# Two weight loads moved among the first rows, an earlier start of weight decoding, and four row loads moved to ScalarE, in an attention and two-layer feed-forward kernel

## The chip, the cores and the metric

The kernel runs on one core of one Trainium2 chip. Its five engines each work through a queue of their own in order: TensorE (PE; its weight loads are shown as PEld), VectorE (DVE), ScalarE (ACT), GpSimd (POOL) and SyncE (SP), which here only issues DMAs. The metric is the device time of one execution in microseconds. Three runs of the kernel before gave 977.05 us as their median (972.66 to 978.73).

## The reference

```python
def _attn_ref(q, k, v):                       # 4 batches, 8 heads, 576 positions, 64 wide
    # out_up: attention among means of 4 positions, repeated 4 times
    # out_local: attention of each position to those less than 4 away
    return (out_up + out_local).astype(np.float32)

x = attn_out.transpose(0, 2, 1, 3).reshape(2304, 512)
h = x @ w_in;  x = (h * sigmoid(h)) @ w_out          # w_in 512 x 2048, w_out 2048 x 512
h = x @ w_in2; out = elu(h) @ w_out2                 # the second layer, same sizes
```

Queries and keys are drawn about six times larger than a tenth of a normal draw. The weights come as 64-bit floats, read here as pairs of 32-bit words.

## The kernel before, in words

A *pair* is two heads of one batch, four pairs to a batch. `attention(i)` is a generator that does one pair in 19 steps: the rows of queries and keys are transposed on TensorE (tile `pst`, L297) and copied to SBUF by ScalarE (L305, L307); the local scores (`psl`, L319) get the mask on VectorE (L326) and their maxima are taken off on GpSimd (`E`, L334); the averaged scores (`psd`, L363) go through exponentials on ScalarE (L377), the local ones too (L383); sums and reciprocals come from VectorE, the products with them from GpSimd; the weights are transposed again (`psE`, `psD`, copies `aT` L406 and `aD` L415 on ScalarE), multiplied with the values (`psu` L422, `pso` L434) and added up in `x32` (L425 ScalarE, L442 VectorE).

A *weight* here is one tile of 128 x 512 numbers, 512 KB as it comes. `load_next` issues its DMA on SP into one of three staging buffers (`ws`). `decode_w` makes a 32-bit float of it: two ScalarE operations (L157, L159), three of VectorE (L168, L169, L175); after the third, the staging buffer is free and the next load is issued. `split_w` cuts it into a high and a low part (ScalarE cast L185, GpSimd L187). The first 16 weights, eight of `w_in` and eight of `w_out` in turn, are all that the first pass of the first layer needs. They are prepared by `prepare_first`, six calls of `small_first` for a weight.

Before the first product of the feed-forward part, a loop runs the four pairs of the first batch (`pending(0)`), counting their steps in `n`. From the thirteenth step on (L722) each step also adds 1.1 to `early`, and every whole unit of it is one call of `small_first`. After that loop come the blocks of 256 tokens. A *unit* is one block with one of eight slices f: `g1` makes `ph` (L501), ScalarE takes the tanh (L518), VectorE the product (L520), ScalarE the high part `gh` (L528), GpSimd the low part; `g2` (L565) follows three units later. The remaining pairs are stepped between the products by `tick`, but only once all 16 first weights have been begun (`first["next"] == 2 * FP`), and what is left of the first weights is stepped there too.

The order on each queue is the order of the code (`manual_schedule`). On SP that is: queries and keys of pairs 0 to 3, the first weight, values of pair 0, the second weight, values of pair 1, the third weight, values of pairs 2 and 3; then each further weight when its buffer is free. Keys of pairs 0 and 1 are issued by ScalarE. Rows of pair 4, the first of the second batch, are loaded by `load_pair` within pair 3's sixth step (L344), on SP.

Every DMA takes the next of eight completion semaphores, in the order of the program whichever engine issues it, and its issue waits until the DMA that had this semaphore before has landed. Below these are called lanes; in lists with waits they are named `DMAHW0` to `DMAHW7`.

Of the kernel before, what the change touches and what calls it, by code (L numbers as in the profile page):

```python
# [22 lines left out]
def attention_moe_moe2_kernel(ctx, tc, q, k, v, wi1, wo1, wi2, wo2, out):  # L23
    nc = tc.nc
# [7 lines left out]
    NPAIR = H // 2  # L32
# [21 lines left out]
    EARLY_PACE = 1.1  # L54
# [73 lines left out]
    def load_next():  # L128
        if at["load"] < len(order):
            load_w(at["load"])  # L130
            at["load"] += 1

    def load_w(i):
        layer, f, which = order[i]
        src = wsrc[layer][which].bitcast(I32)
        st = stage.tile([P, 2 * DM], I32, tag="ws", name="ws", bufs=3)
        if which == 0:
            nc.sync.dma_start(
                st.rearrange("p (c f) -> p c f", c=KC),
                src[:, f * 2 * P:(f + 1) * 2 * P].rearrange("(c p) f -> p c f", p=P),  # L140
            )
        else:
            nc.sync.dma_start(st, src[f * P:(f + 1) * P, :])
        wst[i] = st
# [59 lines left out]
    def load_rows(i, which, engine=None):  # L204
        b, h0 = pairs[i][0], 2 * pairs[i][1]
        src = (q, k, v)[which]
        if which == 2:

            if i < NPAIR:
                heads = [wpool.tile([P, DM], F32R, tag=tag, name="rows2").bitcast(F32) for tag in ("wh0", "wl0")]  # L210
            else:
                t = nat.tile([P, 4 * FAC * D], F32, tag="natv", name="rows2", bufs=1)
                heads = [t[:, :DM], t[:, DM:]]
            for j, t in enumerate(heads):
                (engine or nc.sync).dma_start(t[:HS], src[b, h0 + j].rearrange("(p r) d -> p (r d)", r=2 * FAC))
            loaded[i, which] = heads
            return

        if i in (1, 2):
            ts = [xs.tile([P, NBM], F32R, tag=("xh", "xl")[which], name=f"rows{which}", bufs=6).bitcast(F32) for _ in range(2)]  # L220
            half = NTB // 2
            for j in range(2):
                for a in range(2):
                    (engine or nc.sync).dma_start(
                        ts[a][:TB, :half * 2 * D].rearrange("p (c e) -> p c e", c=half)[:, :, j * D:(j + 1) * D],
                        src[b, h0 + j].rearrange("(c p) d -> p c d", p=TB)[:, a * half:(a + 1) * half],
                    )
                borrowed[2 * i - 2 + which, j] = ts[j]
            loaded[i, which] = [t[:, c * 2 * D:(c + 1) * 2 * D] for t in ts for c in range(half)]
            return  # L230
        elif i == 3 and which == 0:
            borrowed["y"] = yp.tile([P, 4 * NBM], F32, tag="y", name="rows0")
            t = borrowed["y"]
        else:
            t = nat.tile([P, NTB * 2 * D], F32, tag="nat", name=f"rows{which}", bufs=2)
        t = t[:, :NTB * 2 * D].rearrange("p (c e) -> p c e", c=NTB)
        for j in range(2):
            (engine or nc.sync).dma_start(t[:TB, :, j * D:(j + 1) * D], src[b, h0 + j].rearrange("(c p) d -> p c d", p=TB))
        loaded[i, which] = [t[:, c] for c in range(NTB)]

    def load_windows(i):
        b, h0 = pairs[i][0], 2 * pairs[i][1]
        if i in (2, 3):
            vw = borrowed["y"][:, (i - 2) * NW * D:(i - 1) * NW * D].rearrange("p (n d) -> p n d", d=D)
        else:
            vw = nat.tile([P, NW, D], F32, tag="vw", name="vw")
        for j in range(2):
            rows = v[b, h0 + j]
            nc.sync.dma_start(
                vw[j * WIN:(j + 1) * WIN, :NW - 1, :],  # L250
                bass.AP(tensor=rows.tensor, offset=rows.offset, ap=[[D, WIN], [w0[1] * D, NW - 1], [1, D]]),
            )
            nc.sync.dma_start(vw[j * WIN:(j + 1) * WIN, NW - 1, :], rows[w0[-1]:w0[-1] + WIN, :])
        loaded[i, 3] = vw

    def warm(n):
        pz = ps_h.tile([P, 512], F32, tag="h", name="pz")
        for _ in range(n):
            nc.tensor.matmul(pz, wz[0][:, :P], wz[0][:, :512], start=True, stop=True)

    def load_pair(i):
        for which in range(3):
            load_rows(i, which)
# [18 lines left out]
    def attention(i):  # L282
# [11 lines left out]
        for parts in ([(0, c) for c in range(NTB - 1)], [(1, c) for c in range(NTB - 1)], [(0, NTB - 1), (1, NTB - 1)]):  # L294
# [4 lines left out]
            for which in range(2):  # L299
                n = TB * sum(w == which for w, _ in parts)  # L300
# [40 lines left out]
            nc.gpsimd.tensor_tensor(vt[:HS, 2 * j:2 * j + 2], vn[:HS, :, 0:2, :], vn[:HS, :, 2:4, :], ALU.add)  # L341
        nc.gpsimd.tensor_tensor(vd[:HS], vt[:HS, :, 0, :], vt[:HS, :, 1, :], ALU.add)
        if NPAIR - 1 <= i < len(pairs) - 1:
            load_pair(i + 1)  # L344
        if i >= 2:
            load_windows(i)

# [43 lines left out]
        for x, heads in EDs:  # L391
            n = heads.stop - heads.start
# [34 lines left out]
        for t in range(2):  # L427
            ps = bank("pso")
            for w in range(t * NW // 2, (t + 1) * NW // 2):
                n = a0[w + 1] - a0[w]  # L430
# [163 lines left out]

    with tc.manual_schedule():
        for i in range(NPAIR):
            load_rows(i, 0)
            load_rows(i, 1, nc.scalar if i < 2 else nc.sync)
        load_next()
        load_rows(0, 2)  # L600
        load_windows(0)
        load_next()
        load_rows(1, 2)
        load_windows(1)
        load_next()
# [49 lines left out]
        def small_first():  # L655
            live = first["live"]
            if first["next"] < 2 * FP and (sum(x[1] < 3 for x in live) < 2 and len(live) < 3):
                live.append([prepare_first(first["next"]), 0])
                first["next"] += 1
            if live:  # L660
                x = live.pop(0)
                try:
                    next(x[0])
                    x[1] += 1
                    live.append(x)
                except StopIteration:
                    pass
# [7 lines left out]
        def start_pair():  # L675
            i = state["next"]
            if i < state["limit"]:
                state["live"].append([pairs[i], attention(i), 0])
                state["next"] += 1

        def step(b=B):

            live = state["live"]
            if not live or (len(live) < state["most"] and min(x[2] for x in live) >= state["apart"]):
                start_pair()
            if not live:
                return False

            x = next((x for x in live if x[0][0] <= b), live[0])
            live.remove(x)  # L690
            try:
                next(x[1])
                x[2] += 1
                live.append(x)
            except StopIteration:
                pass
            if state["next"] == NPAIR:
                state["most"], state["apart"] = 3, 6
            return True

        def pending(b):
            return state["next"] < len(pairs) and pairs[state["next"]][0] <= b or any(x[0][0] <= b for x in state["live"])
# [6 lines left out]
        n = 0  # L709
        first_x = split_x(0, 0, 0)  # L710
        done = 0
        early = 0.0
        while pending(0):
            step()

            while done < NPAIR and state["next"] > done and pairs[done] not in [p for p, _, _ in state["live"]]:
                next(first_x)
                done += 1
            n += 1
            if n <= 16:  # L720
                warm(1)
            early += EARLY_PACE if n > 12 else 0  # L722
            while early >= 1:
                early -= 1
                if first["next"] < N_EARLY or len(first["live"]) > 1:
                    small_first()
# [48 lines left out]
        for i in range(len(units) + LAG):  # L775
            if i < len(units):
                layer, ps, n, f = units[i]
# [33 lines left out]
            if i >= LAG:  # L811
# [3 lines left out]
                layer, ps, n, f = u  # L815
# [32 lines left out]
```

## Time and profile before

| what | value |
|---|---|
| median of three runs (lowest, highest) | 977.05 us (972.66, 978.73) |
| the profiled execution, its own time | 978.92 us |
| its span, first to last instruction | 977.1 us |
| mean granted TensorE clock | 0.973 |
| PE, DVE, ACT, POOL busy | 96%, 52%, 45%, 36% of the span |

Times inside the trace count from the first instruction. The own time of the profiled execution is 1.8 us longer than its span. PE's busy share says little of the first tenth, where it waits for the other engines: the page's 40 slices show PE at 6, 5, 8 and 8 tenths in the first four (24.4 us each) and at 9 from there on, with a granted clock of 9, 6, 7 and 7 tenths.

### The profile page before, as it was taken

To read this page: it belongs to the slowest core of one execution; us is meant where nothing else is said; L and a number is where in the kernel's file an instruction comes from. 1 tells how busy PE (TensorE), PEld (TensorE's weight loads), DVE (VectorE), ACT (ScalarE), POOL (GpSimd) and SP (SyncE) were. 2 spreads that over 40 slices of the span, in tenths; PEclk is the share of its full clock that TensorE was granted. 3 is DMA by queue.
4 is the path that set the end of the run, shared out by engine and by line. 5 is a ranking of instruction groups with operands and counts; after the bars stand their busy time and mean duration, and the time that the engine had idled before them with its cause. 6 is when DMAs were issued, how large, how long until landed. Compare 5 with 4: busy or idle time off the path is not lost.

```text
span 977.1 us, 16442 instructions
## 1 busy us (share of the span) xinstructions
PE 935.5 (96%) x6493; PEld 805.0 (82%) x6493; DVE 511.7 (52%) x841; ACT 439.4 (45%) x995; POOL 353.1 (36%) x363
## 2 busy tenths in 40 slices
PE   6588999999999999999999999999999999999998
PEld 3357888999989999988888887888888888888886
DVE  4786554454446776654554367656544544434332
ACT  3686454545536666543434345434333433232221
POOL 3675544455452245322223433222233522222221
PEclk9677999999999999999999999999999999999999
DMA  9775342332212650422221103221101011112021
GB/s 181 168 191 159 85 113 70 85 93 71 79 37 87 177 169 35 126 78 87 65 66 64 44 1 87 87 87 44 65 0 44 1 65 65 44 44 86 1 87 44
DMA packets 93484, 77.60 MB, mean 79 GB/s; under 512 B 61664, under 2 KB 82144, under 8 KB 92384
## 3 DMA queue, kind: packets, MB, share of 16 engines
q1 hardware_dynamic: 91008, 75.97, 27.1%
q8 instruction: 51, 0.84, 0.4%
q10 hardware_dynamic: 2400, 0.59, 0.3%
q14 instruction: 25, 0.20, 0.1%
HBM read 62.39 MB, written 14.16 MB: 78 GB/s over the span
## 4 chain that ended last, share of the span: by engine, by line
PE 62%; ACT 1%; DVE 1%; issue 1%; DMA 0%; SPq 0%; DVEq 0%; ACTq 0%
PE ph L501 31%; PE y L567 19%; PE y L565 12%; DMA ws<-in_moe_w_out_dram 0%; DVE part L588 0%; DVE t L523 0%; ACT t L524 0%; ACT xh L462 0%; DVE xl L465 0%; ACT ws L159 0%; ACT gh L528 0%; ACT wf L157 0%; ACT wh L185 0%; DVE wf L169 0%; DVE wf L168 0%
## 5 line engine op out<-in xcount | busy, mean ns | idle before, releaser
L530 POOL TENSOR_TENSOR gl<-t,gh 128x256 fp32r<-128x256 f32 (+1 forms) x192 | 204.6, 1066 | 519.3 <-ACT gh L528 464.9
L501 PE MATMUL ph<-xh,wh 128*128 128x256 f32 (+1 forms) x768 | 252.2, 341 | 3.8 <-ACT xh L462 2.2
L501 PE MATMUL ph<-xl,wh 128*128 128x256 f32 (+1 forms) x768 | 250.9, 339 | 1.8 <-DVE xl L465 1.6
L501 PE MATMUL ph<-xh,wl 128*128 128x256 f32 (+1 forms) x768 | 179.8, 339 | 0.0
L501 PEld LDWEIGHTS ph<-xh,wh 128*128 128x128 f32 x768 | 146.5, 191 | 21.6 <-ACT xh L462 2.8
L501 PEld LDWEIGHTS ph<-xl,wh 128*128 128x128 f32 x768 | 146.5, 191 | 19.1 <-DVE xl L465 3.2
L528 ACT CAST gh<-t 128x256 fp32r<-128x256 f32 (+1 forms) x192 | 98.7, 514 | 120.2 <-DVE t L520 67.7
L565 PE MATMUL y<-gh,wh 128*128 128x256 f32 (+1 forms) x448 | 146.1, 326 | 1.3 <-DVE yo L578 1.3
L501 PEld LDWEIGHTS ph<-xh,wl 128*128 128x128 f32 x768 | 129.1, 191 | 15.3 <-issue 0.2
L565 PE MATMUL y<-gl,wh 128*128 128x256 f32 (+1 forms) x448 | 141.2, 315 | 0.0
L565 PE MATMUL y<-gh,wl 128*128 128x256 f32 (+1 forms) x448 | 141.1, 315 | 0.0
L520 DVE SCALAR_TENSOR_TENSOR t<-t,ph 128x256 f32<-128x256 f32 (+1 forms) x112 | 55.3, 494 | 160.3 <-ACT t L518 159.4
L524 ACT ACTIVATE t<-t 128x512 f32<-128x512 f32 (+1 forms) x80 | 47.1, 589 | 195.6 <-DVE t L523 195.6
L523 DVE TENSOR_SCALAR t<-ph 128x512 f32<-128x512 f32 (+1 forms) x80 | 51.0, 637 | 122.3 <-PE ph L501 121.9
L567 PE MATMUL y<-wh,gh 128*128 128x512 f32 x288 | 112.2, 390 | 0.0
L567 PE MATMUL y<-wh,gl 128*128 128x512 f32 x288 | 112.2, 390 | 0.0
L567 PE MATMUL y<-wl,gh 128*128 128x512 f32 x288 | 112.0, 389 | 0.0
L518 ACT ACTIVATE t<-ph 128x256 f32<-128x256 f32 (+1 forms) x112 | 49.6, 443 | 116.4 <-PE ph L501 113.8
L565 PEld LDWEIGHTS y<-gh,wh 128*128 128x128 f32 x448 | 86.3, 193 | 9.7 <-issue 2.1
L465 DVE TENSOR_TENSOR xl<-x,xh 128x256 fp32r<-128x256 f32 (+1 forms) x96 | 69.4, 740 | 45.1 <-ACT xh L462 43.4
L565 PEld LDWEIGHTS y<-gl,wh 128*128 128x128 f32 x448 | 86.4, 193 | 5.0
L565 PEld LDWEIGHTS y<-gh,wl 128*128 128x128 f32 x448 | 86.2, 192 | 5.0
(90 smaller groups left out, 1211.4 us busy)
## 6 DMA issues: line engine op xcount, KB each, us to landing
ws<-in_moe_w_in_dram SPq DMA_DIRECT2D x32, 512.0 KB
ws<-in_moe_w_out_dram SPq DMA_DIRECT2D x32, 512.0 KB
rows<-in_v_dram SPq DMA_DIRECT2D x36, 144.0 KB
yp<-yo SPq DMA_DIRECT2D x10, 512.0 KB
part<-yp SPq DMA_DIRECT2D x10, 512.0 KB
out_dram<-part SPq DMA_DIRECT2D x18, 256.0 KB
yp<-yo SPq DMA_DIRECT2D x4, 1024.0 KB
part<-yp SPq DMA_DIRECT2D x4, 1024.0 KB
```

The lines of the kernel that those rows point to most:

```text
L465: nc.vector.tensor_tensor(lo[c - 1], src[:, c - 1, :], hi[c - 1].bitcast(F32), ALU.subtract)
L501: nc.tensor.matmul(ph[:, :nb], a[:, c, :], b[c], start=m == 0, stop=m == 3 * KC - 1)
L518: nc.scalar.activation(t, h, AF.Tanh, scale=0.5)
L520: nc.vector.scalar_tensor_tensor(t, t, 1.0, h, op0=ALU.add, op1=ALU.mult)
L523: nc.vector.tensor_scalar_min(t, h, 0.0)
L524: nc.scalar.activation(t, t, AF.Exp)
L528: nc.scalar.copy(gh, t)
L530: nc.gpsimd.tensor_tensor(gl, t, gh.bitcast(F32), ALU.subtract)
L565: nc.tensor.matmul(y[d // share][:, h:h + nb], wm[:, sl], gm, start=first and d % share == 0, stop=last, skip_group_check=True)
L567: nc.tensor.matmul(y[d], gm[:, sl], wm, start=first, stop=last)
```

## The change

Three edits. (1) The first two weight loads stand ahead of the rows of pair 1 and of pair 2 in the start of the program; the third stays where it was. (2) `early` grows from the third step on, no longer from the thirteenth. (3) The queries and keys of pair 4 are issued by ScalarE, its values still by SP; for later pairs all stay on SP.

```diff
@@ attention(i) @@
         if NPAIR - 1 <= i < len(pairs) - 1:
-            load_pair(i + 1)
+            load_rows(i + 1, 0, nc.scalar if i < NPAIR else nc.sync)
+            load_rows(i + 1, 1, nc.scalar if i < NPAIR else nc.sync)
+            load_rows(i + 1, 2)
@@ start of the program @@
         for i in range(NPAIR):
+            if 1 <= i < 3:
+                load_next()
             load_rows(i, 0)
             load_rows(i, 1, nc.scalar if i < 2 else nc.sync)
-        load_next()
         load_rows(0, 2)
         load_windows(0)
-        load_next()
         load_rows(1, 2)
@@ loop over the first batch @@
-            early += EARLY_PACE if n > 12 else 0
+            early += EARLY_PACE if n > 2 else 0
```

Line numbers behind L344 are two higher in the changed kernel (L377 is L379 there, L383 is L385, L501 is L503).

SP's queue at the start. Before, the first weight (`ws_137`) stands behind the rows of all four pairs:

```order
L224 DMA rows1_126<-in_k_dram 96x3x64
L238 DMA rows0_131<-in_q_dram 96x6x64 x2
L238 DMA rows1_134<-in_k_dram 96x6x64 x2
L138 DMA ws_137<-in_moe_w_in_dram 128x4x256
L215 DMA rows2_139<-in_v_dram 72x512
```

In the change (`ws_107` is the first weight, `ws_121` the second, `rows0_109` and `rows0_110` are queries of pair 1, `rows0_123` of pair 2):

```order
L238 DMA rows0_101<-in_q_dram 96x6x64 x2
L138 DMA ws_107<-in_moe_w_in_dram 128x4x256
L224 DMA rows0_109<-in_q_dram 96x3x64
L224 DMA rows0_110<-in_q_dram 96x3x64
L224 DMA rows0_109<-in_q_dram 96x3x64
L224 DMA rows0_110<-in_q_dram 96x3x64
L143 DMA ws_121<-in_moe_w_out_dram 128x1024
L224 DMA rows0_123<-in_q_dram 96x3x64
```

The two weights moved ahead of 16 and 18 of SP's row loads; the third weight (`ws_159` in both) still stands behind the values of pairs 0 and 1.

ScalarE's queue behind the last copy of pair 1's transposed rows, before. `ws_137`, `ws_148` and `ws_159` are the first three weights, L377 the exponentials of pair 0 (`rows0_107`, `rows0_108`), L383 those of its local scores, `pst_355` to `pst_417` rows of pair 2:

```order
L307 COPY x32_98<-pst_315 128x96
L377 ACTIVATE rows0_107,sm_301<-psd_305,nm_311 72x144 x2
L305 ACTIVATE x32_98<-pst_355 128x480
L377 ACTIVATE rows0_108,sm_301<-psd_306,nm_324 72x144 x2
L381 ACTIVATE sm_301<-sm_301 72x4
L157 ACTIVATE pw_369<-ws_137 128x512
L159 ACTIVATE ws_137<-ws_137 128x512
L307 COPY x32_98<-pst_377 128x480
L157 ACTIVATE pw_386<-ws_148 128x512
L159 ACTIVATE ws_148<-ws_148 128x512
L383 ACTIVATE E_247<-E_247 128x640
L305 ACTIVATE x32_98<-pst_417 128x96
```

In the change, from the last copy of pair 1 on (`ws_159` is the third weight, `rows0_109` and `rows0_110` are pair 0's exponentials, `pst_380` and `pst_406` pair 2's rows, `ws_295` is the fourth weight):

```order
L305 ACTIVATE x32_98<-pst_332 128x96
L307 COPY x32_98<-pst_332 128x96
L157 ACTIVATE pw_339<-ws_159 128x512
L159 ACTIVATE ws_159<-ws_159 128x512
L379 ACTIVATE rows0_109,sm_315<-psd_319,nm_325 72x144 x2
L305 ACTIVATE x32_98<-pst_380 128x480
L185 CAST wh1_391<-wf_348 128x512
L379 ACTIVATE rows0_110,sm_315<-psd_320,nm_344 72x144 x2
L383 ACTIVATE sm_315<-sm_315 72x4
L307 COPY x32_98<-pst_406 128x480
L385 ACTIVATE E_250<-E_250 128x640
L157 ACTIVATE pw_419<-ws_295 128x512
```

The third weight moved ahead of all of pair 0's exponentials and of pair 2's copies, which stood before it; the first two weights are decoded and the first is cast ahead of this place.

ScalarE's queue at the loads of pair 4, in the change, with waits (`wh0_667` is the cast of the seventh weight, `ws_581` the ninth weight, L427 is L425 of before, the copy of pair 0's upsampled part):

```order
L408 COPY aT_653<-psE_659 128x384 [waits PE_49,Activation_49]
L385 ACTIVATE E_464<-E_464 128x640
L185 CAST wh0_667<-wf_643 128x512 [waits DVE_49]
L238 DMA rows0_677<-in_q_dram 96x6x64 [waits DMAHW1_49]
L238 DMA rows0_677<-in_q_dram 96x6x64 [waits DMAHW3_49]
L238 DMA rows1_680<-in_k_dram 96x6x64 [waits DMAHW5_49,DMAHW0_49]
L238 DMA rows1_680<-in_k_dram 96x6x64 [waits DMAHW0_49]
L157 ACTIVATE pw_702<-ws_581 128x512 [waits DMAHW4_49]
L159 ACTIVATE ws_581<-ws_581 128x512
L427 COPY x32_98<-psu_709 128x576
```

Before, these four DMAs stood on SP between the ninth weight's load and the values of pair 4, and ScalarE went from the seventh weight's decoding to L425. In the change, lane 5 of the third DMA was last given to the load of the tenth weight, lane 0 of the fourth to the first window load of pair 3, which SP issues three DMAs after that weight.

## Rows read from the trace of the kernel before

**Rows 1.** The page's first line: span and instructions.
```profile
span 977.1 us, 16442 instructions
```
**Rows 2.** Windows: stretch and its length; busy PE, PEld, DVE, ACT, POOL; clock; DMA.
```profile
31.15:52.89 21.74, 15.12 (x125) 9.51 (x125) 15.54 (x28) 15.61 (x44) 13.97 (x16) 0.66 0.65 167
52.89:74.08 21.19, 16.60 (x210) 11.68 (x207) 18.79 (x37) 19.20 (x48) 14.48 (x15) 0.79 0.72 173
74.08:96.16 22.08, 18.41 (x151) 16.83 (x152) 13.93 (x26) 13.96 (x38) 12.60 (x14) 0.77 0.58 166
96.16:130.00 33.84, 31.51 (x413) 28.56 (x412) 18.62 (x41) 17.24 (x59) 18.47 (x23) 1.00 0.33 80
130.00:977.00 847.00, 835.45 (x5400) 727.58 (x5398) 428.62 (x679) 362.81 (x784) 281.83 (x269) 1.00 0.22 69
```
**Rows 3.** Timeline of ScalarE (start, length, what, idle before): the first three weights.
```profile
19.29 0.62 ACT L157 ACTIVATE pw<-ws 128x512 f32<-128x512 f32 x1 [3.02 <-DMA ws<-in_moe_w_in_dram]
...
25.53 0.62 ACT L157 ACTIVATE pw<-ws 128x512 f32<-128x512 f32 x1 [4.60 <-DMA ws<-in_moe_w_out_dram]
...
31.15 0.63 ACT L157 ACTIVATE pw<-ws 128x512 f32<-128x512 f32 x1 [3.02 <-DMA ws<-in_moe_w_in_dram]
```
**Rows 4.** Timeline of ScalarE: attention work, one weight's decoding, and casts.
```profile
26.64 0.72 ACT L383 ACTIVATE E<-E 128x640 f32<-128x640 f32 x1
27.27 0.23 ACT L305 ACTIVATE x<-pst 128x96 f32<-128x96 f32 x1
...
27.51 0.62 ACT L185 CAST wh<-wf 128x512 fp32r<-128x512 f32 x1
...
32.27 0.36 ACT L377 ACTIVATE rows<-psd,nm 72x144 f32<-72x144 f32 x1
...
32.98 0.56 ACT L305 ACTIVATE x<-pst 128x480 f32<-128x480 f32 x1
33.43 0.61 ACT L185 CAST wh<-wf 128x512 fp32r<-128x512 f32 x1
33.94 0.38 ACT L377 ACTIVATE rows<-psd,nm 72x144 f32<-72x144 f32 x1
...
34.92 0.54 ACT L307 COPY x<-pst 128x480 f32<-128x480 f32 x1
```
**Rows 5.** Timeline of SP's queue: issue start and length.
```profile
23.61 0.59 SPq L138 DMA_DIRECT2D ws<-in_moe_w_in_dram  x1
...
42.49 0.39 SPq L138 DMA_DIRECT2D ws<-in_moe_w_in_dram  x1
...
49.52 1.05 SPq L238 DMA_DIRECT2D rows<-in_q_dram  x2
50.66 1.43 SPq L238 DMA_DIRECT2D rows<-in_k_dram  x2
```
**Rows 6.** Windows in which the DMA engines fall silent behind that weight load.
```profile
45.50:46.00 0.50, 0.50 (x5) 0.42 (x4) 0.50 (x2) 0.00 (x0) 0.19 (x1) 0.50 0.19 68
46.00:46.50 0.50, 0.50 (x2) 0.15 (x1) 0.50 (x2) 0.44 (x2) 0.00 (x0) 0.50 0.00 0
```
**Rows 7.** Timeline of ScalarE: the copy with the longest idle time before it.
```profile
50.74 0.48 ACT L406 COPY aT<-psE 128x384 f32<-128x384 f32 x1 [3.67 <-PE psu L422]
```
**Rows 8.** Waits of PE from 74 to 97 us: total, times, longest.
```profile
PE psl L319 <- ACT qk L307: 2.2, 1, 2.2
...
PE ph L501 <- DVE t L520: 0.7, 1, 0.7
```
**Rows 9.** Timeline of VectorE, then of ScalarE, ahead of these two waits.
```profile
79.29 0.69 DVE L168 TENSOR_SCALAR pw<-pw 128x512 f32<-128x512 f32 x1
...
82.42 0.62 ACT L157 ACTIVATE pw<-ws 128x512 f32<-128x512 f32 x1
```
**Rows 10.** Windows of the first block in which PE's clock was low.
```profile
74.49:78.50 4.01, 4.01 (x20) 3.97 (x21) 3.84 (x7) 2.97 (x7) 2.04 (x3) 0.59 0.48 150
...
84.50:92.50 8.00, 6.31 (x63) 5.30 (x63) 6.21 (x11) 3.27 (x11) 5.45 (x6) 0.57 0.64 150
```

## The prediction, as it was put on record

> **What bounds the kernel now.** I read the page first and then cut the span into stretches at the first place where TensorE feeds on finished weights. [rows 2] has these stretches. From 130 us on TensorE is busy for 835.45 of 847.00 us, from 96.16 to 130 for 31.51 of 33.84, at full clock. An edit among the loads of the start can move nothing there. What can move is the first 96 us: 31.15 to 52.89 (attention on the first batch while the first weights are decoded), 52.89 to 74.08 (the rest of that attention) and 74.08 to 96.16 (the first block of 256 tokens). In the second of these ScalarE is busy for 19.20 of 21.19 us and VectorE for 18.79, more than TensorE (16.60), so ScalarE's queue, which works in order, sets the pace. In the first, ScalarE has 15.61 us of work in 21.74. The profiled execution ran 978.92 us by its own time, 1.87 above the median of 977.05; its span is 977.1 [rows 1]. I add up differences against the span, and put the sum on the median, since what lies outside the span is not touched.
>
> [rows 3] shows how the start goes. ScalarE waits three times for a weight's bytes: 3.02 us until 19.29, 4.60 until 25.53, 3.02 until 31.15. Attention work fills the gaps. The third weight is issued at 23.61 [rows 5] and lands 7.5 us later.
>
> **The first two weights, earlier.** Their DMAs move ahead of 16 and 18 of SP's row loads, so they should land well before 19 us, and the waits for them go. This gains nothing by itself: the third weight stays behind the same loads, the same bytes, on the same queue, so I let it land at 31.15 as before. The rows of pairs 1 to 3 come later by the two loads' transfer; with gaps of 5.6 us between weights that landed in a stream of mixed loads [rows 3], 2 to 5 us is my estimate. That costs nothing as long as ScalarE stands before the third weight anyway; that wait is the cover, and without it I would charge about 2 us for each pair.
>
> **Decoding from the third step on.** Here the third weight's first operation (L157) moves ahead of pair 0's exponentials in ScalarE's queue, and waits for a DMA. Whatever stands behind it waits too: pair 0's exponentials, pair 2's copies, the exponential of the local scores, and behind these TensorE's products with them. Before, all of that was done by 31.15. Now it starts there. Its price goes by the same operations, start to next start [rows 4]: the exponentials of one head 0.71 (32.27 to 32.98), of the other with the sums' scaling 0.98 (33.94 to 34.92), the wide copies 0.45 and 0.54, E 0.63 (26.64 to 27.27), the two narrow copies 0.24: 3.6 us. The cast of the first weight stands ahead of the wait now and costs nothing here.
>
> The stretch from the third weight to pair 0's upsampled copy (L425, L427 in the change) had five decodings and four casts; by the order of the change it has seven and six. A decoding costs ScalarE 1.12 us (31.15 to 32.27) and a cast 0.51 (33.43 to 33.94) [rows 3, 4]; two of each are 3.3 us. These are not new work: they leave the first block later on.
>
> **Four loads on ScalarE.** SP took 2.5 us to issue the same four (1.05 and 1.43) [rows 5]. Part of the second length may be waiting, so I take 2.1 us for ScalarE's own issuing. Then come the lanes. The third DMA has the lane of the tenth weight's load. SP issues that load when VectorE finishes the seventh weight, and the same event releases ScalarE's cast just ahead of the four DMAs. A load of that kind, issued at 42.49, had its bytes between 45.5 and 46.0, where the DMA engines fall silent [rows 5, 6]: up to 3.5 us. ScalarE gets to the third DMA 0.5 + 1.05 = 1.6 us after the release and would stand there for up to 1.9. The fourth has the lane of a window load that SP issues three DMAs later; between nothing and 2.3 us more. I take 2.5 us of waiting, with 0 and 4.2 as ends. Behind it stand the ninth weight's decoding and L427, and behind those TensorE's next products.
>
> A rule of the Trainium skill speaks to this move. The page "DMA: Bandwidth & Descriptors", section "Issuing engines are not separate DMA queues", says that DMAs run on the same 16 DMA engines whichever engine starts them, and that starting them on several engines saves only the sequencer's time to start them, which is usually small. By it the move brings the transfers nothing and charges ScalarE what SP is spared: 2.1 us without the waits, and by it the sum would end 0.5 below the time before, at 976.6, as in the third rival. No row of before shows a DMA issue waiting on ScalarE at this place.
>
> **The stretch from 31.15 to L427.** Work: 15.61 + 3.6 + 3.3 + 2.1 = 24.6 us. To that the 2.5 of lane waits. ScalarE's idle time before was 21.74 - 15.61 = 6.13 us, the largest piece 3.67 us ahead of an `aT` copy that follows TensorE [rows 7]. More work ahead of it fills it in part: I keep 2.2 of 6.13. That makes 29.3, against 21.74: **7.6 later**. Ends: 24.6 with no wait at all (+2.9), and 24.6 + 4.2 + 6.1 = 34.9 (+13.2).
>
> **The stretch to the fourth `xh`.** ScalarE's list is the same in kind and number before and after. With 19.20 of 21.19 us busy there are 2.0 to win at most [rows 2]. VectorE's list, 18.79, holds it from below too. I take **0.7 less** (0 to 2.0).
>
> **The first block.** Before, some weights are still decoded there, and two of its waits come from that. TensorE waits 2.2 us at the local scores of pair 4 for ScalarE's copy (L307), which stands behind a weight's decoding at 82.42, and 0.7 us for L520, which stands behind VectorE's weight steps from 79.29 on [rows 8, 9]. With two weights fewer there, ScalarE has 3.3 us less to do and VectorE about 4 (two times three steps of 0.7). I let both waits go: 2.9 us. The second part is the clock. From 84.50 to 92.50, behind the wait for the copies, the granted clock is 0.57, near the lower of its two levels (1.2 GHz, of 1.2 and 2.4), with TensorE busy for 6.31 of 8 us [rows 10]. The same work at full clock is 3.6 us, so 2.7 are to be had if the wait is gone and the clock stays up. I take 2.0. The low clock at 74.49 to 78.50 [rows 10], behind the idle time at the block's start, stays. Sum: **4.9 less** (1.5, if new waits take the old ones' places, to 5.6).
>
> **Sum.** 7.6 - 0.7 - 4.9 = 2.0 later. The rest of the kernel I put at 0, give or take 1. On the median: 977.05 + 2.0 = **979.0 us**.
>
> **The rivals.**
> *The block gives back little.* TensorE may reach the block with pair 4 starting earlier (its transposes move up by one or two units, since all 16 weights are begun sooner) and wait for ScalarE's copies or the tanh there instead. Then only 1.5 come back: 7.6 - 0.7 - 1.5 = 5.4, 982.5 us. For it: the copies of pair 4 still stand between weights in ScalarE's queue. Against it: there are two weights fewer.
> *ScalarE's idle time is filled.* From 31.15 on ScalarE never waits, as in the next stretch where it already is 91% busy: 2.9 - 0.7 - 4.9 = -2.7, 974.3 us. Against it: the 3.67 us wait hangs on a chain over TensorE and GpSimd that more ScalarE work lengthens [rows 7].
> *The four DMAs cost only their issuing.* The two lanes are free when ScalarE gets there, because its queue is later than VectorE's: 2.0 - 2.5 = -0.5, 976.6 us. For it: seven decodings ahead of it make ScalarE the late one. Against it: the cast just ahead is released by the same step as the load.
> *The slower side: the third weight lands late.* If the moved loads push it back, all behind ScalarE's wait goes back with it, one for one. The nearest row for the size is one gap between weights, 5.6 us (25.53 to 31.15) [rows 3]: 2.0 + 5.6 = 7.6, 984.6 us. It decides above 7.8 us of delay, where the sum passes 1%. Against it: the bytes ahead of it are the same.
> That the change does not do what it says is in all of these: the earlier decoding gets through two weights and then stands before the third, whose bytes come no sooner.
>
> **How the numbers follow.** The forecast, 979.0 with 975 to 982 of its own, gets 0.45; the block that gives back little 0.22; the filled idle time 0.14; the four DMAs at their issuing 0.12; the late third weight 0.07. For 8 in 10 I go from 972, the low end of the filled idle time with the block at its best, to 985.5, which takes in the late weight. About 1%, 9.8 us, is what a measurement of this kernel can tell from no change. Faster than 967.3 needs the best end of every term and more: 0.03. Slower than 986.8 needs the late weight or all waits kept, with a block that gives little back: 0.07. The rest, 0.90, is no change.
>
> **What would show it.** In the changed kernel's trace ScalarE should have one long wait for the third weight, ending near 31 us, with pair 0's exponentials behind it; idle time between the four DMAs of L238 on ScalarE; L427 first at about 60.4; the fourth `xh` near 81; the wait for the copies at the local scores of pair 4 gone or short; a clock near 1 in the second half of the first block, and the point that was 96.16 near 98. I would be wrong if the third weight landed more than 3 us away from 31.15, if ScalarE did not stand before it, or if a stretch behind 130 us moved by more than 1 us.

## The result and the profile after

| | before | the change |
|---|---|---|
| median of 12 runs each (lowest, highest) | 977.62 us (972.66, 981.49) | 986.51 us (979.61, 989.31) |
| ratio to before, 95% interval | | 1.0075 (1.005 to 1.010) |
| the profiled execution, its own time | 978.92 us | 988.12 us |

The ratio, taken round by round, is 7.3 us on the median of before, with 4.9 and 9.8 as the ends. (The two medians alone lie 8.9 apart.) That is slower by 0.5 to 1.0%, on the side that was forecast, but over three times the 2.0 us of the sum. On the 977.05 us that the forecast started from, the ratio gives 984.4, inside the range of 972 to 985.5 and near its upper end; the plain median, 986.51, lies 1.0 above that end. The span of the profiled execution:

```profile
span 986.3 us, 16442 instructions
```

Its windows, in the order of [rows 2]: the stretch from the third weight to pair 0's upsampled copy (L427), from there to the fourth `xh`, from there to the fifth tanh, to the eleventh, and to the end.

```profile
28.21:60.52 32.31, 21.17 (x194) 13.53 (x195) 22.84 (x42) 22.49 (x63) 22.60 (x27) 0.66 0.64 165
60.52:84.18 23.66, 18.82 (x205) 13.40 (x207) 18.86 (x37) 18.84 (x48) 12.15 (x12) 0.66 0.50 140
84.18:103.32 19.14, 15.38 (x182) 14.10 (x183) 12.36 (x24) 10.91 (x34) 11.29 (x14) 0.91 0.65 168
103.32:135.34 32.02, 31.10 (x395) 28.58 (x394) 16.99 (x37) 17.20 (x55) 17.39 (x22) 1.00 0.28 68
135.34:986.20 850.86, 838.71 (x5388) 730.23 (x5386) 427.47 (x679) 363.40 (x786) 281.91 (x269) 0.99 0.22 68
```

The same marks in the trace of before (the fourth `xh` itself starts at 73.78, the fifth tanh at 95.16, the eleventh at 128.33):

```profile
52.89:73.78 20.89, 16.60 (x210) 11.68 (x207) 18.49 (x36) 18.90 (x48) 14.48 (x15) 0.79 0.73 176
73.78:95.16 21.38, 17.41 (x143) 15.83 (x144) 13.80 (x25) 13.26 (x35) 12.60 (x14) 0.76 0.57 164
95.16:128.33 33.17, 30.84 (x408) 27.89 (x407) 17.37 (x38) 17.16 (x58) 17.22 (x22) 1.00 0.36 85
```

The first stretch is 10.6 us longer than its 21.74 of before, the second 2.8 longer, the third 2.2 shorter, the fourth 1.2 shorter. The changed kernel is 7.6 us late at L427 (60.52 against 52.89), 10.4 at the fourth `xh`, 8.2 at the fifth tanh, 7.0 at the eleventh, and 9.2 at the end.

ScalarE's timeline (start, length, what, idle time before), to be held beside [rows 3]:

```profile
8.27 0.63 ACT L157 ACTIVATE pw<-ws 128x512 f32<-128x512 f32 x1 [0.82 <-DMA ws<-in_moe_w_in_dram]
...
13.10 0.63 ACT L157 ACTIVATE pw<-ws 128x512 f32<-128x512 f32 x1 [1.84 <-DMA ws<-in_moe_w_out_dram]
...
15.32 0.23 ACT L307 COPY x<-pst 128x96 f32<-128x96 f32 x1
28.21 0.62 ACT L157 ACTIVATE pw<-ws 128x512 f32<-128x512 f32 x1 [12.66 <-DMA ws<-in_moe_w_in_dram]
...
29.31 0.36 ACT L379 ACTIVATE rows<-psd,nm 72x144 f32<-72x144 f32 x1
```

The first two weights are there early. Then ScalarE stands for 12.66 us before the third, and pair 0's first exponential, which before was done ahead of the first weight, starts at 29.31.

Its queue and its engine at pair 4's loads (ACTq is the issuing of DMAs):

```profile
56.27 0.48 ACT L408 COPY aT<-psE 128x384 f32<-128x384 f32 x1 [3.92 <-PE psu L424]
56.35 0.32 ACTq L238 DMA_DIRECT2D rows<-in_q_dram  x1
56.65 0.74 ACT L385 ACTIVATE E<-E 128x640 f32<-128x640 f32 x1
56.72 0.52 ACTq L238 DMA_DIRECT2D rows<-in_q_dram  x1
57.29 0.61 ACT L185 CAST wh<-wf 128x512 fp32r<-128x512 f32 x1
57.33 2.04 ACTq L238 DMA_DIRECT2D rows<-in_k_dram  x2
59.41 0.63 ACT L157 ACTIVATE pw<-ws 128x512 f32<-128x512 f32 x1 [1.52 <-DMA rows<-in_v_dram]
```

The queue issues the first two while the engine still works on what stands ahead of them, and the next operation waits 1.52 us, for a load of values: the lane that the fourth DMA shares with pair 3's window load.

TensorE's longest wait at the start, and its waits in and behind the first block, beside [rows 8]:

```profile
30.17 0.58 PE L259 MATMUL pz<-zeros 128*128 128x512 bf16 x1 [13.98 <-ACT rows L379]
...
89.61 0.81 PE L319 MATMUL psl<-qk 64*64 64x64 f32 x40 [0.28 <-ACT qk L307]
...
96.27 0.60 PE L297 MATMUL pst<-ident,rows 96*128 96x96 f32 x5 [2.40 <-DMA rows<-in_q_dram]
...
141.77 1.03 PE L297 MATMUL pst<-ident,rows 96*128 96x96 f32 x5 [2.62 <-DMA rows<-in_q_dram]
```

The wait for pair 4's copies fell from 2.15 to 0.28 us. In its place TensorE waits 2.40 us for rows of pair 5 (0.42 before) and 2.62 for rows of pair 8 (none before), and behind the second of these the granted clock is 0.66 for 10 us, between its levels of 1.2 and 2.4 GHz:

```profile
140.00:150.00 10.00, 8.23 (x51) 7.92 (x52) 1.55 (x5) 4.37 (x14) 1.78 (x5) 0.66 0.63 119
```

### The profile page after: what moved, and what is told of

Same layout as the page of the kernel before. It is cut to its first block, busy times and chain, and to the rows that moved or that the text cites. A ratio compares the mean times of both kernels' runs of the same rounds, so it can differ in the third digit from the quotient of the medians.

```text
span 986.3 us, 16442 instructions
## 1 busy us (share of the span) xinstructions
PE 937.7 (95%) x6488; PEld 806.6 (82%) x6493; DVE 510.0 (52%) x841; ACT 439.7 (45%) x995; POOL 352.7 (36%) x363
## 4 chain that ended last, share of the span: by engine, by line
PE 61%; DVE 1%; ACT 1%; issue 1%; DMA 0%; DVEq 0%; ACTq 0%
PE ph L503 30%; PE y L569 19%; PE y L567 12%; DMA ws<-in_moe_w_out_dram 0%; DVE part L590 0%; DVE t L525 0%; ACT t L526 0%; DVE wf L169 0%; DVE wf L168 0%; DVE xl L467 0%; ACT ws L159 0%; ACT gh L530 0%; DVE wf L175 0%; ACT wf L157 0%; ACT wh L185 0%
## 5 line engine op out<-in xcount | busy, mean ns | idle before, releaser
L503 PE MATMUL ph<-xh,wh 128*128 128x256 f32 (+1 forms) x768 | 252.3, 341 | 2.5 <-ACT xh L464 1.2
L503 PE MATMUL ph<-xl,wh 128*128 128x256 f32 (+1 forms) x768 | 251.5, 340 | 1.4 <-DVE xl L467 1.3
L503 PE MATMUL ph<-xh,wl 128*128 128x256 f32 (+1 forms) x768 | 179.0, 337 | 0.0
L503 PEld LDWEIGHTS ph<-xh,wh 128*128 128x128 f32 x768 | 145.9, 190 | 20.6 <-ACT xh L464 1.9
L503 PEld LDWEIGHTS ph<-xl,wh 128*128 128x128 f32 x768 | 146.0, 190 | 19.2 <-DVE xl L467 2.7
L503 PEld LDWEIGHTS ph<-xh,wl 128*128 128x128 f32 x768 | 128.3, 190 | 15.5 <-issue 0.4
```

The lines of the kernel that those rows point to most:

```text
L503: nc.tensor.matmul(ph[:, :nb], a[:, c, :], b[c], start=m == 0, stop=m == 3 * KC - 1)
```

## The experiments

Twelve kernels, each in five rounds beside before, with twelve executions of each (six of two_first). All marks are of one profiled execution each, in us of the span; "weights" are those begun ahead of the first tanh; the last two columns are the ratio to before and what it is on 978 us. A mark and a time in the same row do not belong to the same execution: the profiled one of fourteen is 4.4 us under its kernel's median (979.92, 984.28), that of third_behind 3.7 (980.22, 983.90), that of sixteen 2.9, of act_only 2.8, of loads_three 2.5. And from the eleventh tanh to the end the traces take between 844.8 us (loads_three) and 851.0 (the change). So the marks tell what an edit does to the start; the last few us of a time they don't tell. Of two kernels that were measured in different rounds, the times differ clearly only where their intervals don't overlap.

| run | third weight | pair 0's exponentials | fourth `xh` | weights | eleventh tanh | ratio (interval) | us |
|---|---|---|---|---|---|---|---|
| before | 31.1 | ahead of it | 73.8 | 14 | 128.3 | 1 | 0 |
| the change | 28.2 | 29.3 | 84.2 | 16 | 135.3 | 1.0075 (1.0050 to 1.0100) | +7.3 |
| loads_only | 27.9 | 13.5 | 70.4 | 14 | 124.8 | 0.9985 (0.9958 to 1.0012) | -1.5 |
| early_only | 31.4 | 32.5 | 83.5 | 16 | 134.7 | 1.0069 (1.0040 to 1.0098) | +6.7 |
| act_only | 28.6 | 12.7 | 75.6 | 14 | 130.1 | 1.0018 (0.9995 to 1.0040) | +1.8 |
| sp_again | 27.1 | 28.2 | 79.4 | 16 | 130.9 | 1.0042 (1.0015 to 1.0069) | +4.1 |
| late_decode | 27.6 | 12.8 | 73.3 | 14 | 127.8 | 1.0001 (0.9970 to 1.0031) | +0.1 |
| two_first | 28.0 | 15.8 | 81.6 | 16 | 137.7 | 1.0104 (1.0061 to 1.0146) | +10.2 |
| third_load | 18.3 | 19.4 | 80.7 | 16 | 131.3 | 1.0024 (0.9992 to 1.0056) | +2.3 |
| loads_three | 23.0 | 14.9 | 68.7 | 14 | 123.2 | 0.9929 (0.9903 to 0.9954) | -6.9 |
| fourteen | 27.6 | 28.7 | 80.3 | 14 | 132.7 | 1.0044 (1.0018 to 1.0070) | +4.3 |
| sixteen | 28.1 | 13.6 | 72.1 | 16 | 126.6 | 1.0030 (1.0009 to 1.0050) | +2.9 |
| loads_three_slow | 21.2 | 13.1 | 65.9 | 13 | 121.6 | 0.9954 (0.9928 to 0.9979) | -4.5 |
| third_behind | 28.4 | 16.2 | 74.2 | 14 | 129.9 | 1.0061 (1.0036 to 1.0085) | +6.0 |

### One edit at a time

**Loads alone** (before, with the change's order of loads at the start).

> Only the first two weight loads move; decoding still starts at the thirteenth step and pair 4's rows stay on SP. Theory W (the loss comes from ScalarE standing 12.7 us before the third weight with pair 0's exponentials behind it): those exponentials are ahead of all weights again, the waits of 3.0 and 4.6 us for the first two weights go, the third lands near 28: 1 to 5 us faster than before. Theory R (the loss comes from the rows of pairs 1 to 3, which the two loads push back): 3 to 8 us slower.

1.5 us faster, with 4.1 faster and 1.2 slower as ends: theory R, that late rows cost, falls, and W stands as far as this run goes. The waits for the first two weights are gone; one of 6.68 us is left, for the third:

```profile
17.08 0.61 ACT L157 ACTIVATE pw<-ws 128x512 f32<-128x512 f32 x1
...
18.63 0.63 ACT L157 ACTIVATE pw<-ws 128x512 f32<-128x512 f32 x1
...
27.95 0.63 ACT L157 ACTIVATE pw<-ws 128x512 f32<-128x512 f32 x1 [6.68 <-DMA ws<-in_moe_w_in_dram]
```

**Early decoding alone.**

```
-            early += EARLY_PACE if n > 12 else 0
+            early += EARLY_PACE if n > 2 else 0
```

> Only the start of decoding moves, from the thirteenth step to the third; loads and pair 4's rows are as before. Theory W: ScalarE now stands before all three weights (about 19, 25 and 31 us) with the exponentials of pair 0 behind the last: 8 to 15 us slower than before, and the exponentials start after 31 us. Theory R: within 2 us of before.

6.7 us slower, a little under W's 8 to 15 and far from R's 2. ScalarE's queue stands before all three weights:

```profile
18.77 0.62 ACT L157 ACTIVATE pw<-ws 128x512 f32<-128x512 f32 x1 [10.02 <-DMA ws<-in_moe_w_in_dram]
...
24.95 0.62 ACT L157 ACTIVATE pw<-ws 128x512 f32<-128x512 f32 x1 [4.53 <-DMA ws<-in_moe_w_out_dram]
...
31.43 0.63 ACT L157 ACTIVATE pw<-ws 128x512 f32<-128x512 f32 x1 [4.05 <-DMA ws<-in_moe_w_in_dram]
```

This edit carries nearly all of the loss.

**Pair 4's loads on ScalarE alone.**

```
-            load_pair(i + 1)
+            load_rows(i + 1, 0, nc.scalar if i < NPAIR else nc.sync)
+            load_rows(i + 1, 1, nc.scalar if i < NPAIR else nc.sync)
+            load_rows(i + 1, 2)
```

> Only the four loads of pair 4 move to ScalarE. Theory S (what the trace of the change shows: two of the four are issued while ScalarE still works, and the others cost it 1.6 us): 0 to 2 us slower than before. Theory L (the prediction's term: 2.1 us of issuing and 2.5 us in lanes): 3 to 5 us slower, with ScalarE idle for over 4 us at L238.

1.8 us slower, which fits S, though the interval (-0.5 to +3.9) reaches into L. The trace agrees with L at the place itself: ScalarE waits 4.52 us there.

```profile
48.36 0.52 ACTq L238 DMA_DIRECT2D rows<-in_q_dram  x1
51.13 2.41 ACTq L238 DMA_DIRECT2D rows<-in_k_dram  x2
53.58 0.62 ACT L157 ACTIVATE pw<-ws 128x512 f32<-128x512 f32 x1 [4.52 <-DMA rows<-in_q_dram]
```

**The change without that edit** (its queries and keys of pair 4 back on SP).

> The change with pair 4's queries and keys back on SP. Theory S: 0 to 2 us faster than the change, so 5 to 9 us slower than before. Theory L: 3 to 5 us faster than the change, so 2 to 5 us slower than before.

4.1 us slower than before, 3.2 less than the change: both in L's ranges, and neither in S's, though the interval (1.5 to 6.7) takes in some of S's. From the third weight to the fourth `xh` it takes 52.3 us, the change 56.0, so the edit costs 3.7 there; between loads_only (42.4) and late_decode (45.8) it is 3.4, between before (42.6) and act_only (47.0) 4.3.

**The change without early decoding.**

> The change with decoding from the thirteenth step again: the loads' move and ScalarE's four loads are left. If the parts add up (loads alone -1.5 us, ScalarE's loads alone +1.8): within 2 us of before. If the loads on ScalarE cost more next to the moved weights: 3 to 5 us slower.

0.1 us (-2.9 to +3.0): the two other edits cancel, as the sum of the single runs (-1.5 + 1.8) says. The three single runs add up to 7.0 us, the change has 7.3; each has an interval of 2 to 3 us either way.

### What it is in early decoding that costs

W says: the wait with pair 0's exponentials behind it. F says: two more weights decoded ahead of the first product.

**Exponentials ahead of the third weight, 16 weights.**

```
-                if first["next"] < N_EARLY or len(first["live"]) > 1:
-                    small_first()
+                if first["next"] < (2 if n <= 12 else N_EARLY) or len(first["live"]) > 1:
+                    small_first(2 if n <= 12 else 2 * FP)
```

(`small_first` gets an argument for how many weights may be begun.)

> The change, but only two weights are begun up to step 12, so that the third weight's operation stands behind pair 0's exponentials in ScalarE's queue; 16 weights are still begun ahead of the first tanh, and pair 4's rows are issued by ScalarE. Theory W (the place of the third weight in the queue is what costs): 4 to 8 us faster than the change, within 3 us of before. Theory F (the two further weights that are decoded ahead of the first product cost): within 2 us of the change, 5 to 9 us slower than before.

10.2 us slower (6.0 to 14.3, from six executions), so W in this form falls: the exponentials run at 15.8 and it doesn't help. F said within 2 us of the change; it is 2.9 above it, with intervals that overlap. Behind the wait, now 8.91 us, there still stand pair 2's copy and the local scores' exponential.

**The third weight's load earlier.**

```
-            if 1 <= i < 3:
+            if 1 <= i < 4:
                 load_next()
```

(The `load_next()` behind pair 1's windows goes.)

> The change, with the third weight's load moved up too, ahead of pair 3's queries; queues of the engines that compute are as in the change. Theory W: the 12.7 us wait shrinks to some 5 and the exponentials start about 7 us earlier: 4 to 8 us faster than the change. Theory F: within 2 us of the change.

2.3 us slower than before (from 0.8 faster to 5.5 slower), 5 less than the change, as W said. The third weight is there at 18.26 and the exponentials follow, but the next weight takes the wait over:

```profile
18.26 0.62 ACT L157 ACTIVATE pw<-ws 128x512 f32<-128x512 f32 x1 [3.49 <-DMA ws<-in_moe_w_in_dram]
...
19.36 0.36 ACT L379 ACTIVATE rows<-psd,nm 72x144 f32<-72x144 f32 x1
...
31.83 0.63 ACT L157 ACTIVATE pw<-ws 128x512 f32<-128x512 f32 x1 [6.91 <-DMA ws<-in_moe_w_out_dram]
```

The exponentials come 10 us earlier than in the change, the fourth `xh` only 3.5.

**14 weights instead of 16, third weight in its early place.**

```
-            early += EARLY_PACE if n > 2 else 0
+            early += 0 if n <= 2 else EARLY_PACE if n <= 16 else 0.95
```

> The change, with the early decoding at 0.95 instead of 1.1 a step from the seventeenth step on: 14 weights are begun ahead of the first tanh, as before, and the third weight still stands ahead of pair 0's exponentials. Theory F (the two further weights ahead of the first product cost): 5 to 8 us faster than the change, within 2 us of before. Theory W (ScalarE's wait for the third weight with the exponentials behind it costs): within 2 us of the change, 5 to 9 us slower than before.

4.3 us slower, 3.0 less than the change: neither theory alone. Against late_decode, which has the same loads, the same 14 weights and its third weight at the same 27.6 us, the fourth `xh` is 6.9 us later (late_decode first, then fourteen):

```profile
73.35 0.41 ACT L464 CAST xh<-x 128x256 fp32r<-128x256 f32 x1 [0.97 <-DVE x L444]
80.29 0.43 ACT L464 CAST xh<-x 128x256 fp32r<-128x256 f32 x1
```

That is the price of decoding early with the number of weights kept. The third weight's place is not all that differs: the first two weights are decoded some 8 and 5 us sooner as well. How much of it is the place, third_behind asks.

**16 weights instead of 14, third weight in its late place** (loads_only with a pace of 1.3 instead of 1.1).

> The two loads moved, decoding from the thirteenth step at 1.3 instead of 1.1 a step: 16 weights are begun ahead of the first tanh, and the third weight stands behind pair 0's exponentials; pair 4's rows on SP. Theory F: 5 to 9 us slower than before. Theory W: as with the loads alone, 0 to 4 us faster than before. If each holds half: 2 to 4 us slower.

2.9 us slower, 4.4 more than loads_only: the third reading, that each holds half, has it in its range. But a pace of 1.3 moves all later weights, not two alone, and at the fourth `xh` it costs only 1.8 us (72.1, 70.4), at the first tanh 4.7 (77.63, 72.97).

**Everything of pair 0's front half ahead of the third weight, 14 weights** (as two_first, with 18 in place of 12).

> The change, with no more than two weights begun up to step 18: the third weight's operation stands behind pair 0's exponentials, its local scores' exponential and pair 2's copies, and 14 weights are begun ahead of the first tanh, as in the run with 14 (4.3 us slower than before), in which it stands ahead of all of these. Theory C (what stands behind the third weight is the front of a chain over all engines, which starts only when it lands): the fourth xh comes 5 to 8 us sooner than the 80.3 us there, and the time is 3 to 6 us less, within 2 us of before. Theory D (decoding early costs by the order of its steps on VectorE and GpSimd, wherever the third weight stands): within 2 us of the run with 14.

At the fourth `xh` theory C is right: 74.2 us, 6.1 sooner than fourteen's 80.3. In the time it isn't: 6.0 us slower than before (3.5 to 8.3), within 2 us of fourteen, as theory D said. In the first block TensorE waits 5.00 us for a VectorE step of a weight:

```profile
74.21 0.41 ACT L464 CAST xh<-x 128x256 fp32r<-128x256 f32 x1 [0.39 <-DVE x L444]
...
84.75 1.06 PE L297 MATMUL pst<-ident,rows 96*128 96x96 f32 x5 [5.00 <-DVE wf L175]
```

Here two weights' first operations stand together at 78.75 and 80.38 in ScalarE's queue, and pair 4's transposes take the PSUM bank in which such a weight lies until its third VectorE step. From 84 to 88 us the granted clock is 0.53. At the second tanh the kernel is 2.7 us behind before, at the fourth 5.8, but at the fifth and at the eleventh 1.6 again, and at the end 1.3. So in this trace the wait is made up for the most part: of the lead of 6.1 over fourteen 2.8 is left at the eleventh tanh and nothing at the end (978.4, 978.1). Where the 6.0 us of the time come from, this trace, 3.7 us under the kernel's median, doesn't show.

### A faster version

**Three loads moved, nothing else** (loads_only with the third load ahead of pair 3's queries as well).

> Before with the loads of the first three weights moved up, the third ahead of pair 3's queries; decoding from the thirteenth step, pair 4's rows on SP. If ScalarE's 6.7 us wait for the third weight (seen with two loads moved) sets the end: 3 to 7 us faster than before. If the attention's own chain takes its place: 0 to 3 us faster.

6.9 us faster than before (4.5 to 9.5), the fastest kernel of the study. ScalarE waits for none of the first three weights, as the attention's work runs ahead of them, and 4.23 us for the fourth:

```profile
14.91 0.39 ACT L377 ACTIVATE rows<-psd,nm 72x144 f32<-72x144 f32 x1
...
18.57 0.61 ACT L157 ACTIVATE pw<-ws 128x512 f32<-128x512 f32 x1
...
23.03 0.64 ACT L157 ACTIVATE pw<-ws 128x512 f32<-128x512 f32 x1
...
32.42 0.63 ACT L157 ACTIVATE pw<-ws 128x512 f32<-128x512 f32 x1 [4.23 <-DMA ws<-in_moe_w_out_dram]
```

**The same with fewer weights early** (a pace of 1.0).

> The first three loads moved up, decoding from the thirteenth step at 1.0 a step instead of 1.1 (13 weights begun ahead of the first tanh). If work ahead of the first product is what counts, the first tanh comes 2 to 4 us sooner than the 70.7 us with 1.1 and the time is 0 to 3 us less than that kernel's (7 us under before). If the weights then fall short in the first block: 0 to 4 us more than that kernel's.

4.5 us faster than before, 2.4 less so than with 1.1, as the second alternative had it, though the two intervals overlap. Its reason, that the weights fall short in the block, isn't shown: the fourth `xh` is 2.8 us sooner, the first tanh 0.6, and the eleventh still 1.6 (121.64, 123.20). The two traces part behind it (850.5 and 844.8 us to the end).

## Why the prediction was right in sign and short in size

The sum was 7.6 later at L427, 0.7 less at the fourth `xh`, 4.9 less in the first block, nothing behind it. The traces have 7.6 later at L427, 2.8 more at the fourth `xh`, 2.2 less at the fifth tanh, 1.2 less at the eleventh, and 2.2 more to the end: 9.2. That L427 came at 60.52, where 60.4 was forecast, is luck: the third weight was 2.94 us sooner than assumed, just inside the 3 that were named as a sign of being wrong, and the stretch behind it 3.0 longer. The fourth `xh`, near 81 by the forecast, came at 84.18.

**The first two weights: right.** Their waits shrink from 7.62 us in all to 2.66, and the move alone gives 1.5 us (from 4.1 faster to 1.2 slower). **The third weight at 31.15: off by 2.9 to the good side** (28.21). It was assumed that the loads ahead of it decide, and these stayed. With the loads as before it was first used at 31.1, 31.4 and 28.6 us in three kernels; in the eight kernels that moved the first two loads and left the third, at 27.1 to 28.4, sooner than in any of the three. It was issued at nearly the same time (23.61 before, 23.80 in the change). One reading is that the second weight's bytes, which before were still awaited until 25.53, were down by 13.10 in the change and shared the way no longer; no run tried that alone.

**Decoding ahead of pair 0's exponentials: right in mechanism, too small.** 3.6 us of ScalarE's work was charged. Between late_decode and fourteen it costs 6.9 us at the fourth `xh`. What waits is the front of a chain through VectorE, GpSimd and TensorE (TensorE stands 14 us, from 16.2 to 30.2, in the change), and the chain's own waits begin only when ScalarE gets through. The sum priced the work that moves behind the third weight on ScalarE alone; in the first stretch VectorE is busy for 7.3 us more than before, GpSimd for 8.6 and TensorE for some 6, the two further weights' steps included. The runs show the delay; third_behind, where moving that front half back gives 6.1 us at the fourth `xh`, more than the 3.6, speaks for the chain against ScalarE's load alone, but its order and pace of later weights differ too, and its time doesn't follow.

**Two more weights ahead of the first product: right.** 3.3 us were charged; from the third weight to the fourth `xh` the change takes 56.0 us and fourteen 52.7, which is 3.3. Between sixteen and loads_only it is 1.7.

**ScalarE's loads: near.** 2.1 of issuing and 2.5 of lanes were charged, 3.4 to 4.3 us are measured at the fourth `xh`, counted from the third weight, by three pairs of runs. The range of the lanes had a window load's wait of up to 2.3 us in it that no row gave. The parts were wrong: the first two DMAs are issued beside ScalarE's work and cost it nothing, and what costs is the wait behind the lanes, 1.5 to 4.5 us. The rule of the Trainium skill that was weighed ("DMA: Bandwidth & Descriptors", section "Issuing engines are not separate DMA queues") has only the issuing time as a price; the waits in these traces stand outside it.

**ScalarE's idle time filled by the new work: this step failed.** "I keep 2.2 of 6.13" took 3.9 us off, and the next stretch 0.7 more. In the first stretch ScalarE's work is 22.49 us, as charged without the loads (15.61 + 3.6 + 3.3 = 22.5), but its idle time went up, from 6.13 to 9.82 us, and the wait ahead of `aT` stayed (3.92 us, [rows 7] 3.67). In the second, where ScalarE's queue was to set the pace, it is busy for 18.84 of 23.66 us (18.90 of 20.89 before) and waits for TensorE's transposes (`psE`) for 4.2. TensorE has nearly the same list there, 205 instructions against 210, and takes 18.82 us at a clock of 0.66 for it, where it took 16.60 at 0.79. That the lower clock makes the 2.8 us is likely by these rows; no run tested it. The upper end that was given for the first stretch alone (+13.2) had all idle time kept; the 10.6 measured lie a little nearer to it than to the 7.6. By the runs the way from the third weight to the fourth `xh` is 42.6 us before, 45.8 in late_decode (the two sets of moved loads), 52.7 in fourteen (decoding early) and 56.0 in the change (two more weights). These are steps from one kernel to the next, so they add up whatever their causes; they show where the 13.4 us go.

**The first block: half.** 4.9 us were to come back; 2.2 did by the fifth tanh. The wait for pair 4's copies goes and the clock is 0.91 instead of 0.76, as forecast. But rows of later pairs are then late: pair 5's for 2.40 us at 96.27, and pair 8's for 2.62 at 141.77 with ten microseconds at a granted clock of 0.66 behind. SP issues pair 5's queries at 90.31, behind three weight loads, and pair 8's at 137.61, behind a store of `yo` (L595):

```profile
84.61 5.65 SPq L138 DMA_DIRECT2D ws<-in_moe_w_in_dram  x3
90.31 2.11 SPq L238 DMA_DIRECT2D rows<-in_q_dram  x2
...
137.15 0.36 SPq L595 DMA_DIRECT2D yp<-yo  x1
137.61 1.34 SPq L238 DMA_DIRECT2D rows<-in_q_dram  x2
```

This is the first rival (the block gives back little, new waits in the old ones' place); it named ScalarE's copies or the tanh, and it was rows. That these waits are what keeps the change at 7 to 9 us is read from the trace; no run took them away alone. The wait for pair 5 is not peculiar to the change: loads_three, the fastest kernel, has one of 2.18 us. The wait for pair 8 goes with sixteen weights: all six kernels that begin 16 ahead of the first tanh have it, at 2.59 to 2.66 us; of the eight others two have it, with 0.17 and 1.74.

**The rest of the kernel at 0, give or take 1: this failed too.** A stretch behind 130 us that moves by more than 1 was named as a sign of being wrong. From the eleventh tanh to the end the change takes 2.2 us more than before, with the wait for pair 8 in it. sixteen, which has that wait, is 1.7 us ahead of before at the eleventh tanh and 0.4 behind at the end of its trace; but traces without it differ from before there by more (loads_three and fourteen take 4.0 and 3.4 us less), so how much of the 2.2 is the wait stays open.

What stays open: why two_first is slower than the change by ratio (1.0104 and 1.0075, with intervals that overlap) although its fourth `xh` is 2.6 us sooner. By its eleventh tanh it is 2.3 us later than the change, so the loss lies in the first two blocks. It has the wait that third_behind has, for L175 of a weight ahead of pair 4's transposes, with 2.94 us; whether that makes the loss was not tried.

## What to carry to other kernels

In an in-order queue an operation that waits for a DMA is better placed behind what is already ready: here that was worth 6.1 us at the end of the stage, though not in the time, which has to be read again for each order. A start made earlier in the code is worth nothing before its bytes are there, and here moving one more load (6.9 us faster) did what decoding earlier (6.7 us slower) couldn't. Idle time of a waiting engine may be charged as filled only where its waits don't hang on a chain that the new work pushes back: keep it in the sum, and take the filled case as the end of the range. A gain at the start of a stage isn't one in the time until the stage's own waits are read again.

## What was not expected of the hardware

ScalarE's queue issued two DMAs (0.32 and 0.52 us) while its engine ran the copy and the exponential ahead of them, so issuing on a computing engine cost 0 where nothing waited, and 1.5 to 4.5 us where a completion lane did. The same third weight, behind the same loads on the same queue, was used first at 31.1, 31.4 and 28.6 us in the executions of three kernels, a spread as large as most terms of this sum; in eight kernels in which the first two weights were moved ahead, it was used at 27.1 to 28.4.
